# Step orders of a recurrent attention kernel laid anew, and the late pass of its first expert moved into the ordered part

## The chip, the cores and the metric

The kernel runs on one core of a Trainium2 chip. The metric is the device time of one execution in microseconds (us). The core has five engines with a queue each: TensorE (PE, matmuls; PEld is its loading of weights), VectorE (DVE), ScalarE (ACT), GpSimd (POOL) and SyncE (SP, which here only issues DMAs).

## The reference

Two blocks. The first is a recurrence over 768 tokens for 4 batches of 8 heads of 40 columns, the second sends each of the 3072 tokens through one of 8 experts:

```python
for t in range(S):
    y[:, :, t] = np.einsum('bhd,bhde->bhe', rt, state)
    Sa = np.einsum('bhde,bhe->bhd', state, at)
    state = state * wt[:, :, None, :] - np.einsum('bhd,bhe->bhde', Sa, bt) + np.einsum('bhd,bhe->bhde', vt, kt)
...
logits = x @ w_gate
expert_idx = np.argmax(logits, axis=1)
for e in range(E):
    h = np.maximum(x_sorted[lo:hi] @ w1[e], 0.0)
    y_sorted[lo:hi] = h @ w2[e]
return gate_w[:, None] * y_sorted[inv_perm]
```

All is float32. An expert has w1 of 320 x 1024 and w2 of 1024 x 320.

## The kernel before, in words

**Units.** The recurrence is done in chunks of 64 tokens. A unit is one chunk of two batches (16 heads), so there are 24 units, numbered 0 to 23. `unit(u)` lists its steps: loads of the six inputs (`load`, L793), two scans over the decays on DVE (`scan_r`, `scan_q`), the scaling of the inputs (`decay_kb`, `decay_a`), a product of the scaled inputs on PE (`p_a`), the inverse of a triangular matrix by repeated squaring (`p_sq`, `p_sum2`, `p_sum4`, `p_sum8`, `p_last`, with the copies `x0`, `x1`, `s1` and so on between them), the right-hand side and the solution (`p_rhs`, `p_first`, `p_q`, `p_u2`), the output and the new state (`p_z`, `p_y`, `sa`), and transposes on PE (`t_v`, `t_kb`, `t_gt`, `t_st`, `t_u`). `p_x` turns the output into rows of tokens and computes the gate's logits; the rows are scaled (`scaled`, `weight`) and written to `x_rows` in DRAM (`store`). A name with `:21` is that of unit 21; `/1` is the second step of that name in the unit.

**Routing.** Every few units `route` picks the expert of each token (`choose`), counts (`p_count`, `counts`, `place`) and builds a table of the tokens of each expert (`one_hots`, `p_table`, `tab`). From it come index tables: `rows_from` (where to gather rows) and `rows_to` (where to scatter results). `by_count` and `in_places` sort the experts 1 to 7 by size, which the fetch of weights after `order` needs.

**Expert 0 in the ordered part.** Expert 0 has room for 448 rows. Its first 256 are taken from the early chunks: gathered by two `rows_in` (POOL), transposed (`p_rows`, L1353, copied by `rows`), through layer 1 (`p_h`, `p_h3` for the last 64 input columns, `relu`) and layer 2 (`p_z0`), copied to `zo` and scattered by `rows_out` (L330). Six more `rows_in` gather the 192 late rows of expert 0 (`/2`, `/3`) and the rows of expert 1 (`/4` to `/7`).

**Order.** Each step is declared with its engine, its cost by the author's estimate, what it reads and writes, and `n`, the number of records that it puts into PE's queue (a matmul counts as two matmuls and two weight loads). `in_order()` (L483) then emits everything. On each engine the order is written out by hand: `FIRST_STEPS` for the start, `LAST_STEPS` for the end, and between them `CYCLE`, which gives each step a place relative to its unit, so that the same order comes back for each unit. The planner in `in_order` keeps a clock, which decides PSUM banks and how many dummy matmuls (`keep_warm`, L479) go into PE's gaps of the first 60 us and ahead of the labels in `KEEP`. It models PE's instructions as coming in pages of `PAGE` = 256 records, of which a new one may start `FETCH` us after the one before it at the earliest. Into these pages it counts only `n`.

**The second part.** After the ordered part its pool of buffers (`ring`) and its PSUM pool are given back, and the rest is scheduled by the framework: at its head the late pass of expert 0, `layer1` on the 192 late rows into `h_first` (L1461, L1469, L1475, L1476) and `layer2` of 128 of them (L1486, L1492); then experts 1 to 7, PE busy with layer 1 and layer 2 in turn, while POOL gathers the next experts' rows (`gathers`, L1439) and SP fetches their weights (L318, L320, L324). `wx`, one large tile, holds the X buffers of the ordered part and later the weights and rows of expert 1. `xg`, `h_first` and the weights of expert 2 lie where the ring was.

Of the kernel before, what the change touches and what calls it, by code (L numbers as in the profile page):

```python
# [23 lines left out]
def kernel(  # L24
# [249 lines left out]
    def rows_to_(v, t, tmp, gi, si):  # L274

        ta, tb, ia, ib = tmp
        v.tensor_scalar(ia, gi, scalar1=(B - 1) * C, scalar2=None, op0=ALU.bitwise_and)
        v.tensor_scalar(ib, gi, scalar1=(B * C).bit_length() - 1, scalar2=None, op0=ALU.arith_shift_right)
        v.tensor_copy(tb, gi)
        v.scalar_tensor_tensor(tb, in0=ia, scalar=float(NCH - 1), in1=tb, op0=ALU.mult, op1=ALU.add)  # L280
        v.scalar_tensor_tensor(tb, in0=ib, scalar=float(C - B * C), in1=tb, op0=ALU.mult, op1=ALU.add)

        v.tensor_scalar(ta, t, scalar1=0.0, scalar2=float(2 * N), op0=ALU.is_equal, op1=ALU.mult)
        v.tensor_tensor(si, tb, ta, op=ALU.add)
# [44 lines left out]
    def rows_out(zo, si, alone=False):  # L329
# [5 lines left out]
        if not alone:  # L335
# [8 lines left out]
    PAGE, FETCH, FIRST = 256, 3.6, 190  # L344
# [5 lines left out]
            t_v:0 t_kb:0 p_a:0 p_sq:0 t_v:1 t_kb:1 t_gt:0 p_sum2:0 p_a:1 p_sum4:0 p_sq:1 p_sum8:0 t_gt:1 p_rhs:0 p_last:0 p_sum2:1 p_q:0 p_a:2  # L350
            p_first:0 p_sum4:1 p_u2:0 t_u:0 p_sum8:1 p_z:0 p_rhs:1 p_last:1 p_sq:2 t_kb:2 p_y:0 p_sum2:2 p_q:1 p_first:1 t_gt:2 t_kb:3 p_u2:1 t_v:2
            p_sum4:2 t_u:1 p_a:3 p_z:1 p_sum8:2 p_sq:3 p_y:1 p_last:2 t_gt:3 p_x:0 p_rhs:2 p_sum2:3 p_q:2 p_first:2 p_x:1 p_u2:2 t_st:2 t_v:3
            p_sum4:3 p_a:4 t_u:2 t_kb:4 p_sum8:3 p_z:2 p_sq:4 p_last:3 t_v:4 t_st:3 p_rhs:3 p_y:2 t_v:5 p_sum2:4 p_q:3 t_kb:5 p_x:2
        """,
        DVE: """
            zero_dec zero/3 zero/1 zero_dec/1 scan_r:0 zero_dec/2 decay_kb/1:0 recip:0 scan_q:0 decay_a:0 scan_r:1 recip:1 decay_kb/1:1 n1:0 n1/1:0
            t1:0 scan_r:2 x0:0 s1:0 scan_q:1 decay_a:1 x02:0 s2/1:0 recip:2 n1:1 s2:0 n1/1:1 t1:1 x04:0 s4/1:0 s4:0 s1:1 scan_q:2 s8/1:0 x08:0 s8:0
            x0:1 direct/1:0 direct:0 apart:0 s2:1 decay_kb/1:2 s2/1:1 x02:1 n1:2 n1/1:2 t1:2 s4:1 x04:1 s4/1:1 scan_r:3 recip:3 x08:1 s8/1:1 s8:1
            zu/1:0 zu:0 scan_r:4 s1:2 x0:2 direct/1:1 direct:1 xt:0 x02:2 decay_kb/1:3 s2:2 s2/1:2 scan_q:3 scan_r:5 x04:2 s4/1:2 s4:2 n1/1:3 n1:3
            t1:3 zu/1:1 zu:1 s8:2 x08:2 s8/1:2 recip:5 xt:1 s1:3 kept/1:2 x0:3 recip:4 scan_q:4 x12/1:3 x02:3 s2:3 logits:0 logits:1 s2/1:3  # L360
            weight:0 weight:1 u/1:2 scaled:1 minus:2 s4:3 x04:3 x14/1:3 s4/1:3 n1:4 n1/1:4 t1:4 x08:3 s8/1:3 s8:3 zu:2 kept/1:3 zu/1:2 v:4 scan_r:6
            apart/1:3 s1:4 x0:4 sa:2 xt:2 scan_q:5 x12:4 nkb/1:5 s2:4 x02:4
        """,
        ACT: """
            zero/4 first_load/1:0 first_load/3:0 first_load/3:1 first_load/1:1 zero/5 zero/7 pc:0 zero/10 nkb/1:0 zero/8 nkb:0 pc:1 gt/1:0 zero/9
            gt:0 off/1:0 pc:2 v/1:0 v:0 x1:0 nkb/1:1 off:0 gk:0 x12/1:0 gt:1 x12:0 zero/6 nkb:1 gt/1:1 x14:0 x14/1:0 x1:1 off/1:1 off:1 v/1:1 rhs:0
            v:1 apart/1:0 x12:1 x12/1:1 q:0 gk:1 first:0 x14:1 minus:0 x14/1:1 off:2 u:0 ut:0 gt:2 off/1:2 gt/1:2 u/1:0 rhs:1 x1:2 nkb/1:2 nkb:2
            pc:3 apart:1 apart/1:1 sa0:0 x12:2 q:1 first:1 x12/1:2 gk:2 nkb:3 minus:1 nkb/1:3 v/1:2 ut:1 pc:4 v:2 x14/1:2 x14:2 u:1 gt:3 u/1:1
            off/1:3 gate/6 gt/1:3 x1:3 off:3 kept:2 sa0:1 gk:3 apart:2 apart/1:2 rhs:2 pc:5 q:2 first:2 x12:3 exp:0 exp:1 u:2 sn:2 v:3 v/1:3 x14:3
            scaled/1:1 scaled:0 gt:4 scaled/1:0 ut:2 off/1:4 gt/1:4 off:4 nkb/1:4 nkb:4 kept:3 x1:4 sn:3 rhs:3 v/1:4 apart:3 v:5 x12/1:4 q:3  # L370
        """,
        POOL: """
            zero/11 zero basis basis/1 zero/2 const gate const/1 basis/2 const/2 basis/3 basis/4 const/3 basis/5 basis/6 const/4 const/5 basis/7
            const/6 basis/8 basis/9 basis/10 basis/11 basis/16 basis/12 zero/12 decay_kb:0 const/7 basis/17 basis/13 const/8 zero/13 basis/14
            const/9 basis/15 const/10 const/11 blocks zero/19 basis/18 decay_kb:1 const/12 const/13 zero/15 const/14 gt_mask:0 basis/19 gate/1
            zero/17 zero/14 const/15 gate/2 const/16 gate/3 const/17 gt_mask:1 const/18 basis/20 const/19 const/20 const/21 decay_a:2 decay_kb:2
            basis/21 gate/4 gt_mask:2 const/22 const/23 zero/16 decay_kb:3 decay_a:3 const/24 zero/18 decay_kb/1:4 zero/20 const/25 st:2 gt_mask:3
            decay_kb:4 tt_add:2 decay_kb/1:5 decay_a:4 xs_pad:0 st:3 gt_mask:4 decay_kb:5 tt_add:3 decay_kb:6 decay_kb/1:6 decay_a:5 st:4 const/26
            xs_pad:1
        """,  # L380
        SP: """
            first_load:0 first_load/2:0 first_load/5:0 first_load/4:0 first_load:1 first_load/2:1 load:2 first_load/5:1 first_load/4:1 load/1:3
            load/2:2 load/3:2 load/1:2 load/3:4 first_load/6:0 load:5 load:3 gate/5 load/2:3 load:4 load/3:3 load/4:3 first_load/6:1 load/2:4
            load/4:2 load/1:4 load/1:5 load/5:2 load/2:6 load/1:6 load/4:4 load/2:5 load/3:5 load:6 load/4:5 load:7 store:0 load/5:3 load/2:7
            load/1:7 load/3:6 store:1 load:8 load/5:4
# [4 lines left out]
            t_gt:21 t_st:20 p_q:20 p_first:20 p_sum4:21 p_u2:20 p_a:22 p_sum8:21 t_u:20 p_x:19 p_z:20 p_last:21 p_rhs:21 t_gt:22 p_sq:22 p_y:20  # L390
            p_q:21 p_sum2:22 p_first:21 t_kb:23 p_u2:21 p_sum4:22 p_a:23 p_x:20 p_rhs:22 p_sum8:22 t_u:21 p_count:19 p_sq:23 p_last:22 p_z:21
            t_st:22 t_st:21 t_v:23 p_sum2:23 p_y:21 p_rows p_sum4:23 p_q:22 p_first:22 p_x:21 t_gt:23 p_u2:22 p_sum8:23 p_rhs:23 t_u:22 p_last:23
            t_st:23 p_z:22 p_q:23 p_first:23 p_u2:23 p_table:19 p_rows/1 t_u:23 p_y:22 p_z:23 p_h p_count:21 p_x:22 p_y:23 p_h/1 p_h/2 p_x:23
            p_h/12 p_h/13 p_h/3 p_count:23 p_h3 p_h/14 p_table:21 p_h/15 p_h/4 p_h/5 p_h/6 p_table:23 p_h/7 p_h3/1 p_h3/3 p_h/8 p_h/9 p_h/10 p_z0/8
            p_h/11 p_h3/2 p_z0 p_z0/1 p_z0/2 p_z0/9 p_z0/10 p_z0/3 p_z0/11 p_z0/12 p_z0/4 p_z0/5 p_z0/13 p_z0/6 p_rows/4 p_rows/3 p_z0/14 p_rows/5
            p_z0/7 p_rows/6 p_rows/2 p_z0/15 p_rows/7
        """,
        DVE: """
            x12/1:21 s2/1:21 x04:21 s4/1:21 s4:21 n1/1:22 n1:22 t1:22 s8:21 x08:21 s8/1:21 logits:19 zu/1:20 zu:20 kept/1:21 weight:19 apart/1:21
            x0:22 s1:22 xt:20 scan_q:23 x02:22 s2:22 s2/1:22 sa:20 s4:22 x04:22 n1/1:23 s4/1:22 n1:23 x14/1:22 t1:23 logits:20 s8/1:22 s8:22 x08:22  # L400
            x0:23 direct:22 direct/1:22 s1:23 zu/1:21 zu:21 weight:20 x12:23 s2:23 x02:23 s2/1:23 sa:21 xt:21 s4:23 x04:23 rows s4/1:23 x14/1:23
            s8:23 s8/1:23 x08:23 rhs:23 direct:23 direct/1:23 apart/1:23 sn:23 q:23 logits:21 zu/1:22 zu:22 choose:21 weight:21 scaled:21
            scaled/1:21 xt:22 zu/1:23 zu:23 place:21 logits:22 xt:23 one_hots:21 tab:19 logits:23 choose:23 weight:23 weight:22 place:23
            one_hots:23 tab:21 scaled:22 tab:23 rows_from:23 by_count:23 in_places:23 rows_from/1:23 rows/6 rows/2 zo rows_to:23 rows_to:15
        """,
        ACT: """
            apart:20 apart/1:20 nkb:22 v/1:22 x12:21 gk:21 v:22 q:20 first:20 sn:20 x14/1:21 x14:21 minus:20 u/1:20 u:20 ut:20 off:22 gt/1:22 gt:22
            off/1:22 kept:21 exp:19 rhs:21 scaled:19 gk:22 scaled/1:19 apart:21 pc:22 x1:22 q:21 x12:22 first:21 x12/1:22 minus:21 u:21 u/1:21
            nkb:23 nkb/1:23 x14:22 off:23 gt:23 rhs:22 gt/1:23 off/1:23 counts:19 ut:21 apart/1:22 x1:23 exp:20 sn:21 apart:22 scaled/1:20 sn:22
            x12/1:23 v/1:23 v:23 scaled:20 first:22 q:22 x14:23 gk:23 minus:22 ut:22 apart:23 first:23 minus:23 exp:21 ut:23 rows/1 exp:23 exp:22  # L410
            scaled/1:22 relu relu/1 scaled/1:23 scaled:23 relu/2 relu/6 relu/3 relu/4 relu/5 relu/7 rows/4 rows/5 rows/7 zo/1 rows/3
        """,
        POOL: """
# [1248 lines left out]
```

## Time and profile before

| | |
|---|---|
| median of 3 runs | 660.93 us (659.87 to 661.71) |
| the profiled execution | 665.98 us, span 664.2 us |
| mean granted PE clock | 0.992 |
| PE busy, 0 to 17, 17 to 60 us | 11.44 of 17, 36.23 of 43 us |
| PE busy, 100 to 400 us | 94.38, 95.19 and 94.47 us of each 100 |
| PE busy, 420 to 440, 440 to 460 us | 14.08 and 20.00 of 20 us, clock 0.87 and 0.96 |
| PE busy, 600 to 664.2 us | 56.37 of 64.2 us |
| instruction queue q8 | 105 packets, 1.72 MB |
| last matmul of the ordered part, first of expert 1 | before 431.6 us, at 447.39 us |

Times in the profile are from the start of the span. "x13256" is a count of instructions; in a timeline row the figures are start, duration, engine, line, operation, output and inputs, count, and in brackets the idle time before it with what ended it. "issue" is idle time in which the engine waited for nothing that the profile shows. PEclk is the clock that TensorE was granted, as a share of full speed.

### The profile page before, as it was taken

The page shows a single profiled execution, that of the slowest core. Times are in us where ns is not written, and L with a number is a line of the kernel's source. Part 1 is how long each engine was busy: PE and PEld are TensorE (multiplying, and loading weights), DVE is VectorE, ACT ScalarE, POOL GpSimd, SP SyncE. Part 2 cuts the span into 40 slices and gives each one's busy share as a digit, 9 for nine tenths or more (in the row PEclk, how much of TensorE's full clock was granted, in tenths as well). Part 3 has the DMA queues.
Part 4 walks back from the last instruction along what each step waited for, and adds up shares of the span by engine and source line. Part 5 has one row for each costly group of instructions (what it writes and reads, how often), then busy time and mean ns, then how long its engine had stood idle before and what let it go on. Part 6 is the DMA issues. An engine that isn't in the chain of part 4 may idle for free. (4 is left out here: it accounts for less than half of the span.)

```text
span 664.2 us, 30511 instructions
## 1 busy us (share of the span) xinstructions
PE 620.6 (93%) x13256; PEld 491.5 (74%) x13256; DVE 377.6 (57%) x906; ACT 291.1 (44%) x778; POOL 276.0 (42%) x426
## 2 busy tenths in 40 slices
PE   6699999999999999999999999789999999999995
PEld 6588888888898888888888887564656566555663
DVE  6898988778888888888887777312011201111110
ACT  5567666566676766676667542101010111101010
POOL 8625535565656465737565430250105013111101
PEclk9999999999999999999999999889999999999998
DMA  4433233233333434333332211764528212135000
GB/s 102 91 80 86 63 82 82 64 76 76 80 81 85 104 87 104 83 83 95 74 99 71 72 39 38 229 217 134 178 95 260 76 34 59 42 114 156 20 10 26
DMA packets 120189, 60.55 MB, mean 91 GB/s; under 512 B 100571, under 2 KB 115934, under 8 KB 120052
## 3 DMA queue, kind: packets, MB, share of 16 engines
q1 hardware_dynamic: 115036, 48.83, 27.9%
q0 software_dynamic: 2976, 9.24, 4.3%
q8 instruction: 105, 1.72, 1.1%
q10 hardware_dynamic: 2040, 0.49, 0.3%
q14 instruction: 32, 0.26, 0.1%
HBM read 49.88 MB, written 8.94 MB: 89 GB/s over the span
## 5 line engine op out<-in xcount | busy, mean ns | idle before, releaser
L1475 DVE TENSOR_SCALAR h_sb<-hp 128x416 f32<-128x416 f32 (+3 forms) x28 | 16.3, 582 | 164.8 <-PE hp L1469 141.6
L756 PE MATMUL ps<-wx 64*64 64x96 f32 (+1 forms) x3072 | 83.9, 241 | 5.0 <-issue 2.9
L330 POOL DMA_INDIRECT out_dram<-zo,s_idx x24 | 23.7, 988 | 143.8 <-ACT zo L1492 142.6
L756 PEld LDWEIGHTS ps<-wx 64*64 64x64 f32 x3072 | 68.4, 133 | 13.9 <-issue 5.6
L883 DVE TENSOR_TENSOR wx<-ps,wx 64x128 f32<-64x128 f32 (+1 forms) x216 | 61.7, 286 | 16.6 <-PE ps L756 11.2
L915 DVE STREAM_TRANSPOSE wx<-ps 128x512 f32<-128x512 f32 x72 | 51.1, 710 | 20.7 <-PE ps L756 17.3
L825 POOL TENSOR_TENSOR KB<-KB,rv 128x512 f32<-128x512 f32 x44 | 52.6, 1213 | 9.9 <-DMA KB<-in_packed_dram 4.5
L745 ACT COPY wx<-ps 128x256 f32<-128x256 f32 (+2 forms) x116 | 45.6, 419 | 25.1 <-PE ps L1353 13.1
L855 POOL TENSOR_TENSOR GT<-GT,m_low 128x512 f32<-128x512 f32 x24 | 30.6, 1277 | 58.7 <-ACT GT L853 29.1
L1492 ACT COPY zo<-zp 128x320 f32<-128x320 f32 (+1 forms) x24 | 10.2, 425 | 102.0 <-PE zp L1486 94.2
L1476 ACT ACTIVATE h_sb<-hp 128x416 f32<-128x416 f32 (+3 forms) x28 | 14.3, 509 | 86.5 <-PE hp L1469 43.5
L1486 PE MATMUL zp<-wx,h_sb 128*128 128x320 f32 (+3 forms) x176 | 48.5, 433 | 0.0
L1461 PE MATMUL hp<-xgT,w 128*128 128x416 f32 (+1 forms) x128 | 46.6, 512 | 0.0
L1486 PE MATMUL zp<-w,h_sb 128*128 128x320 f32 (+1 forms) x176 | 44.1, 433 | 0.0
L756 PE MATMUL ps<-ZU,nKB 128*64 128x104 f32 (+1 forms) x768 | 40.6, 254 | 2.6 <-issue 2.5
L1486 PEld LDWEIGHTS zp<-wx,h_sb 128*128 128x128 f32 (+3 forms) x176 | 30.5, 175 | 13.8 <-issue 0.7
L945 POOL TENSOR_TENSOR Tb<-Tb,wx 128x256 f32<-128x256 f32 x20 | 18.2, 908 | 51.2 <-ACT Tb L745 41.4
L1461 PEld LDWEIGHTS hp<-xgT,w 128*128 128x128 f32 x128 | 23.7, 190 | 21.2 <-issue 17.1
L756 PEld LDWEIGHTS ps<-ZU,nKB 128*64 128x64 f32 x768 | 34.6, 137 | 5.7 <-issue 4.1
L1486 PEld LDWEIGHTS zp<-w,h_sb 128*128 128x128 f32 (+1 forms) x176 | 28.8, 175 | 13.3 <-issue 0.7
L827 POOL TENSOR_TENSOR A<-A,q 128x512 f32<-128x512 f32 x22 | 26.9, 1222 | 24.8 <-DVE q L818 21.3
L818 DVE TENSOR_TENSOR_SCAN q<-dec,qini 128x520 f32<-128x520 f32 x24 | 35.9, 1496 | 0.2
(282 smaller groups left out, 1394.9 us busy)
## 6 DMA issues: line engine op xcount, KB each, us to landing
KB<-in_packed_dram SPq DMA_DIRECT2D x184, 40.0 KB
w<-in_moe_w_dram SPq DMA_DIRECT2D x10, 512.0 KB
w<-in_moe_w_dram SPq DMA_DIRECT2D x16, 320.0 KB
x_rows<-xs SPq DMA_DIRECT2D x24, 192.0 KB
Vu<-in_packed_dram SPq DMA_DIRECT2D x96, 40.0 KB
A<-in_packed_dram SPq DMA_DIRECT2D x96, 40.0 KB
R<-in_packed_dram SPq DMA_DIRECT2D x96, 40.0 KB
wx<-in_moe_w_dram SPq DMA_DIRECT2D x12, 320.0 KB
```

The lines of the kernel that those rows point to most:

```text
L330: ins_ = nc.gpsimd.indirect_dma_start(out=out[:, :], out_offset=bass.IndirectOffsetOnAxis(ap=si, axis=0), in_=zo, in_offset=None, bounds_c ...
L745: nc.scalar.copy(dst, src)
L756: nc.tensor.matmul(out_, lhsT=lhsT, rhs=rhs, start=start, stop=stop, skip_group_check=True)
L818: Step(turn_of("scan_q", pre - 1.0), DVE, 1.26, lambda e: nc.vector.tensor_tensor_scan(qq[:], dec[:, : SEG * C1], qi[:].rearrange("p s j - ...
L825: Step(turn_of("decay_kb", pre), on_, 1.2 if on_ == POOL else 0.65, lambda e, kb=kb, by=by: any_(e).tensor_tensor(kb, kb, by, op=ALU.mult) ...
L827: Step(turn_of("decay_a", pre), DVE if early else POOL, 0.65 if early else 1.2, lambda e: any_(e).tensor_tensor(Aq[:], Aq[:], q3[:, :, :C] ...
L855: Step(turn_of("gt_mask", rk), POOL, 1.28, lambda e, d=dst_, m=mask: nc.gpsimd.tensor_tensor(d, d, m, op=ALU.mult), reads=[h_basis], write ...
L883: nc.vector.tensor_tensor(dst[o_, q, :, 2, :HB], src[o_, q, :, 1, :HB], old[o, q, :, 2, :HB], op=ALU.add)
L915: Step(turn_of(f"x0{k}", rk - 0.4), DVE, 0.72, lambda e, ps=ps, Xn=Xn: nc.vector.transpose(Xn[:, :, :, 0, :], half_sums(ps, 2)[:, :, :, 0, ...
L945: Step(turn_of("tt_add", rk - 1.5), POOL, 0.72, lambda e, X=X, Tb=Tb: nc.gpsimd.tensor_tensor(Tb[:], Tb[:], X[:, :, :, 2, :HB], op=ALU.add ...
L1461: nc.tensor.matmul(hps[i][:, : c1 - c0], lhsT=w[0][:, db, (fb + i) * 128 : (fb + i + 1) * 128], rhs=xT[:, db, c0:c1], start=(db == 0 and n ...
L1486: nc.tensor.matmul(zp[r0 : r0 + n], lhsT=h[:, fb, c0 : c0 + n], rhs=w[2][:, fb, :], start=(fb == 0), stop=(fb == FB - 1), skip_group_check ...
```

## The change

1. **The page count.** `FETCH` goes from 3.6 to 3.7. The planner now also counts into the pages four records per dummy matmul, and the extra records of some steps (`MORE`).
2. **All step orders are new**: FIRST_STEPS, LAST_STEPS and CYCLE. In one unit PE did `p_last t_kb p_rhs t_v t_gt p_sum2 p_q p_first p_a p_u2 p_sum4 t_st t_u p_x p_z p_sq p_sum8 p_y`; it does `p_last t_kb t_v p_rhs p_sum2 p_q t_gt t_st p_first p_a p_u2 p_sum4 t_u p_x p_z p_sum8 p_sq p_y`. `counts` goes from ACT to DVE.
3. **The late pass of expert 0 becomes ordered steps**: `p_hb`, `p_hb3`, `relu_late` (two per block of 128 hidden columns), `p_zb`, `zo_late` and a third `rows_out`. Its hidden values go to `late_h`, over the second KB buffer, and for the 64 rows that wait for expert 1 to `h_tail` in `wx`. `h_first` is gone.
4. **`zo` of the early rows** moves from the ring's `rv` buffers to `wx`; `zo_late` lies over `turn_gate`.
5. **`rows_to` of the early rows** is cut into seven steps named `to`, declared when their table is ready instead of at the end.

The core of the diff, with the PE rows of the lists and the POOL and SP rows that matter:

```diff
-    PAGE, FETCH, FIRST = 256, 3.6, 190
+    PAGE, FETCH, FIRST = 256, 3.7, 190
+    MORE = {"t_v": 2, "p_a": 1, "p_sq": 1, "p_z": 2}
...
     FIRST_STEPS = {
         SP: """
-            first_load:0 first_load/2:0 first_load/5:0 first_load/4:0 first_load:1 first_load/2:1 load:2 first_load/5:1 first_load/4:1 load/1:3
+            first_load:0 first_load/2:0 first_load:1 first_load/4:0 first_load/2:1 load:2 first_load/5:0 first_load/4:1 load/1:2 load/2:2
...
     LAST_STEPS = {
         PE: """
-            t_st:23 p_z:22 p_q:23 p_first:23 p_u2:23 p_table:19 p_rows/1 t_u:23 p_y:22 p_z:23 p_h p_count:21 p_x:22 p_y:23 p_h/1 p_h/2 p_x:23
-            p_h/12 p_h/13 p_h/3 p_count:23 p_h3 p_h/14 p_table:21 p_h/15 p_h/4 p_h/5 p_h/6 p_table:23 p_h/7 p_h3/1 p_h3/3 p_h/8 p_h/9 p_h/10 p_z0/8
-            p_h/11 p_h3/2 p_z0 p_z0/1 p_z0/2 p_z0/9 p_z0/10 p_z0/3 p_z0/11 p_z0/12 p_z0/4 p_z0/5 p_z0/13 p_z0/6 p_rows/4 p_rows/3 p_z0/14 p_rows/5
-            p_z0/7 p_rows/6 p_rows/2 p_z0/15 p_rows/7
+            t_st:23 t_u:22 p_h p_h/1 p_h/2 p_q:23 p_first:23 p_count:21 p_h/3 p_h3 p_u2:23 p_z:22 t_u:23 p_table:19 p_h/12 p_h/13 p_z:23 p_y:22
+            p_y:23 p_h/8 p_x:22 p_h/9 p_table:21 p_h/10 p_h/4 p_x:23 p_h/5 p_h/6 p_h/14 p_h/11 p_count:23 p_h/7 p_h/15 p_h3/1 p_h3/3 p_h3/2 p_z0/8
+            p_table:23 p_z0/9 p_z0 p_z0/1 p_z0/10 p_z0/2 p_z0/11 p_z0/12 p_z0/13 p_z0/3 p_z0/4 p_z0/5 p_z0/6 p_z0/14 p_rows/3 p_rows/2 p_z0/15
+            p_z0/7 p_hb p_hb/1 p_hb/12 p_hb/4 p_hb/8 p_hb/5 p_hb/6 p_hb/7 p_hb/9 p_hb/10 p_hb/13 p_hb/14 p_hb/11 p_hb/2 p_hb/15 p_hb/3 p_hb3
+            p_hb3/1 p_hb3/2 p_hb3/3 p_zb p_rows/4 p_zb/1 p_zb/2 p_rows/5 p_zb/3 p_zb/4 p_rows/6 p_zb/5 p_zb/6 p_rows/7 p_zb/7
...
         POOL: """
-            rows_in/1 xs_pad:21 xs_pad:22 xs_pad:23 rows_in/3 rows_in/4 rows_in/5 rows_in/6 rows_in/7 rows_in/2 rows_out rows_out/1
+            xs_pad:20 xs_pad:21 xs_pad:23 xs_pad:22 rows_in/3 rows_in/2 rows_in/4 rows_in/7 rows_in/5 rows_in/6 rows_out/1 rows_out/2 rows_out
...
     CYCLE = {
-        "p_a": [(PE, -2.325)], "p_count": [(PE, 2.025)], "p_first": [(PE, -0.375)], "p_last": [(PE, -0.725)], "p_q": [(PE, -0.425)], "p_rhs": [(PE, -0.625)],
-        "p_sq": [(PE, -1.875)], "p_sum2": [(PE, -1.475)], "p_sum4": [(PE, -1.225)], "p_sum8": [(PE, -0.825)], "p_table": [(PE, 5.075)], "p_u2": [(PE, -0.275)],
+        "p_a": [(PE, -2.475)], "p_count": [(PE, 1.875)], "p_first": [(PE, -0.525)], "p_last": [(PE, -0.975)], "p_q": [(PE, -0.725)], "p_rhs": [(PE, -0.825)],
+        "p_sq": [(PE, -2.075)], "p_sum2": [(PE, -1.775)], "p_sum4": [(PE, -1.375)], "p_sum8": [(PE, -1.175)], "p_table": [(PE, 5.425)], "p_u2": [(PE, -0.425)],
...
-            left = s.n
+            warm = 0
+            if s.n and new and idle > 0.9 and (t < WARM or s.label in KEEP):
+                warm = int((idle - (0.6 if idle < 8 else 3.0)) / 0.3)
+            left, done = s.n, -4 * warm - MORE.get(s.name, 0) if s.n else 0
...
-            while left:
+            while left or done:
...
             if c1 == EC:
-                later.append(found(0, tab_a[:], g0_idx[:], s0_idx[:], [h_tab_a]))
+                found(0, tab_a[:], g0_idx[:], s0_idx[:], [h_tab_a])
+                for part in rows_to_parts(nc.vector, tab_a[:], [x[:, :NA] for x in tmp], g0_idx[:], s0_idx[:]):
+                    Step(turn_of("to", rk), DVE, 0.18, lambda e, part=part: part(), reads=[h_idx[0], h_tab_a], writes=[h_to[0], h_itmp])
...
-                later.pop()()
...
+        h_tail = wx[:, : FB * (CAP - EW - 128)].rearrange("x (k r) -> x k r", k=FB)
...
-        zo0 = [(t[:, :Dm], held) for t, held in r_rv.bufs]
+        late_h = flat(r_KB.bufs[1][0]).rearrange("x (k r) -> x k r", k=FB)
+        zo_late, hzo_late = flat(turn_gate)[:, :Dm], [h_tg]
+        zo0 = [(wx[:, tail_w + i * Dm : tail_w + (i + 1) * Dm], [part_of(r_X.bufs[0][1])]) for i in range(NA)]
...
+        for fb in range(0, FB, 2):
+            ps = Held(2)
+            for i in range(2):
+                for db in range(DB - 1):
+                    Step(late + 2, PE, 0.33, lambda e, ps=ps, fb=fb + i, i=i, db=db: mm(
+                        psum[:, ps.at + i, : CAP - EW], w0[0][:, db, fb * 128 : (fb + 1) * 128], xT0[:, db, EW:], start=(db == 0), stop=False,
+                    ), reads=hxT_late + [h_w], writes=[ps], n=4, lag=0, shape=WHOLE, name="p_hb")
...
+            if j == NA:
+                for fb in range(FB):
+                    Step(late + 3, PE, 0.54, lambda e, ps=ps, fb=fb: mm(
+                        psum[:, ps.at, :Dm], late_h[:, fb], w0[2][:, fb, :], start=(fb == 0), stop=(fb == FB - 1),
+                    ), reads=late_parts[0][fb : fb + 1] + [h_w], writes=[ps], n=4, shape=WHOLE, lag=0.2 if fb + 1 == FB else 0, name="p_zb")
+                Step(late + 3, ANY, 0.42, lambda e, ps=ps: copy(e, zo_late, psum[:, ps.at, :Dm]), reads=[ps], writes=hzo_late, name="zo_late")
+                Step(late + 3, POOL, 1.2, lambda e: rows_out(zo_late, s_idx[:, NO - 1 : NO]), reads=hzo_late + [h_to[2]], lag=2.5, name="rows_out")
+                continue
...
-    hs[0] = wk_pool.tile([128, FB, CAP - EW], F32, name="h_first", bufs=1)
-    layer1(weights[0], xTs[0], hs[0], EW, CAP, to=0)
-    layer2(rows_to(0, 0), (weights[0], hs[0], 0, 128))
```

## The prediction

> **What bounds the kernel now.** First the page's busy shares and the time in 40 slices, then the windows by stage: TensorE (PE) is busy 93% of the span, 284 of the 300 us from 100 to 400, and all of 440 to 600. The other engines stay under 60%. So time can come only from PE's own gaps and from its slow clock.
>
> ```profile
> PE 620.6 (93%) x13256; PEld 491.5 (74%) x13256; DVE 377.6 (57%) x906; ACT 291.1 (44%) x778; POOL 276.0 (42%) x426
> ```
>
> Second, who PE waits for in the ordered stage (60 to 400 us):
>
> ```profile
> PE ps L756 <- issue: 11.6, 26, 1.2
> PE ps L756 <- ACT wx L745: 1.5, 9, 0.2
> ```
>
> "issue" means that no semaphore held it. The timeline shows where:
>
> ```profile
> 204.93 0.48 PE L756 MATMUL ps<-ZU,nKB 128*64 128x104 f32 x5 [0.47 <-issue]
> 212.80 0.83 PE L756 MATMUL ps<-x,Q 64*64 64x40 f32 x22 [0.79 <-issue]
> ...
> 228.24 0.90 PE L756 MATMUL ps<-x,Q 64*64 64x40 f32 x25 [0.23 <-issue]
> ```
>
> The gaps fall inside a step, between equal matmuls. From 204.93 to 212.80 there are about 254 matmul records and as many weight loads, so two pages of 256 in 7.87 us; the later gaps at 236.41, 244.05, 251.96 and 259.71 are again about 7.8 us apart. PE is waiting for its instructions, in one page of every two. How much that is per unit:
>
> ```profile
> 107.74 1.09 PE L984 MATMUL ps<-ident,KB 128*128 128x128 f32 x8
> 348.36 1.09 PE L984 MATMUL ps<-ident,KB 128*128 128x128 f32 x8
> ```
>
> This step comes once per unit: 15 units in 240.62 us, 16.04 us each. Third, the end of the ordered stage:
>
> ```profile
> 419.47 2.85 PE L756 MATMUL ps<-w,dec 128*128 128x320 f32 x10
> 425.04 1.54 PE L1353 MATMUL ps<-ident,q 128*128 128x128 f32 x6 [2.71 <-DMA q<-x_rows,g_idx]
> ...
> 431.61 1.57 PE L1461 MATMUL hp<-xT,w 128*128 128x192 f32 x8 [0.96 <-ACT xT L745]
> ...
> 437.74 2.37 PE L1461 MATMUL hp<-xT,w 128*128 128x192 f32 x8 [2.21 <-ACT h_first L1476]
> ...
> 443.08 4.47 PE L1486 MATMUL zp<-w,h_first 128*128 128x320 f32 x16
> 447.39 3.17 PE L1461 MATMUL hp<-wx 128*128 128x448 f32 x8
> ```
>
> Three stops, and after two of them the same 192-column step takes 2.37 us instead of 1.57. The granted clock says why (in the windows, the figure after the length and five busy times: 0.67, 0.50, 0.59):
>
> ```profile
> 424.00:426.00 2.00, 0.96 (x5) 0.96 (x6) 0.00 (x0) 0.02 (x1) 0.00 (x0) 0.67 1.05 370
> 426.00:428.00 2.00, 2.00 (x8) 1.50 (x7) 0.00 (x0) 0.46 (x1) 0.00 (x0) 0.50 1.01 351
> ...
> 438.00:440.00 2.00, 2.00 (x8) 1.60 (x7) 0.33 (x2) 0.00 (x0) 1.70 (x2) 0.59 0.78 248
> ```
>
> What the third stop waits for is in the chain and on GpSimd (POOL): row scatters from rv start only after the last index chain of VectorE (DVE), and h_first lies where the ring was, so its first write waits until the second scatter has read rv.
>
> ```profile
> 434.43 1.00 DMA out_dram<-rv,s_idx
> 435.43 1.62 issue
> ```
> ```profile
> 433.10 1.03 POOL L330 DMA_INDIRECT out_dram<-rv,s_idx  x1 [10.14 <-DVE s_idx L284]
> ```
>
> **The late pass (p_hb, p_hb3, p_zb).** Before, PE's last early matmul ends at 422.32 and expert 1 starts at 447.39: 25.07 us. The same work by its warm rows, start to start: six p_rows at 0.45 = 2.7; three p_z0 at 0.54 = 1.6; layer 1 of 192 columns 4 x 1.50 = 6.0; its third part 2 x 0.85 = 1.7; layer 2 447.39 - 443.08 = 4.3; sum 16.3. The last evacuation (zo_late, 0.42 like the other zo copies, with its hand-over about 0.7) now stands ahead of the first hp, which takes the banks. 17.0, so 8.1 us can go. The other edits here cost no PE time: rows_to in seven DVE pieces of 0.16 us leaves the end of the chain for gaps far earlier, zo moves to wx, so nothing of the ring waits for a scatter.
>
> What is late next. (a) All sixteen p_h now stand ahead of p_table:23, and p_x:23 has ten p_h and one p_h3 before it instead of three p_h: about 4 us later, at 410.3 for 406.3. The index chain, the gathers of experts 0's late rows and 1's rows and the 2.56 MB fetch of expert 1 (issued 414.60 to 419.7, DMA full until 428.5) shift with it, to about 432.5. Expert 1 would start near 440, its transposes p_rows/4 to 7 near 434: covered by p_hb and p_zb; without that cover this would be a wait of up to 4 us. (b) p_rows/3 and /2 now stand ahead of p_hb. Their two gathers are now the first on POOL, ahead of the weights in time (about 417 to 419 against 420). Bounds: nothing, if they land as free transfers; 4.6 us, if rows_in/2 takes the 7.1 us that rows_in/4 took (issued 416.91 to 417.9, used at 425.04 in a full DMA). I take 1.0, nearer nothing, since their issue is ahead. (c) On POOL rows_out/2 stands ahead of rows_out and of the seven gathers of experts 2 and 3; it waits for zo_late. They start near 443 instead of 437.93, 3 us after expert 1's start instead of 9.5 ahead of it. PE wants the first four 15.8 us after that start (463.22 - 447.39), they are issued by 448 and may take 7.1 us: about 1.5 us of slack. The Trainium skill (DMA: Bandwidth & Descriptors, the arbitration rule of the queue model) has each engine take turns between its queues, packet by packet, which would bring them in 2 to 3 us, a cost of nothing; the 7.1 us row would eat the slack. I take 0.5, bounds 0 and 3. DVE and ScalarE (ACT) have 16 small relus more in the list, but they stand for the eight of h_first (0.33 to 0.36 each), while PE has p_zb; nothing.
> Late pass: 25.1 - 17.0 - 1.5 = **-6.6** (bounds -8.1 and -0.5).
>
> **The step orders.** The set of PE steps per unit is unchanged, 1024 records and by the new table 6 more; only the sequence changes. Durations start to start from 216.23 to 231.73: p_z 1.16, p_sq 0.68, p_sum8 0.66, p_y 2.04 (its 0.47 stall out), p_last 0.60, t_kb 1.02, p_rhs 1.07, t_v 0.49, t_gt 0.53, p_sum2 0.72, p_q 0.46, p_first 0.44, p_a 0.90, p_u2 0.80, p_sum4 0.70, t_st 0.49, t_u 0.45, p_x 1.00: 14.2 us, against 16.04 measured. Cut into pages of 256 from p_z on, the old order takes 2.50, 4.06, 3.09 and 4.56 us. If no page may follow in less than 3.7 us (the new FETCH; two pages at 7.64 to 7.9 us in the trace allow it), the unit is 3.7 + 4.06 + 3.7 + 4.56 = 16.0. That meets the trace. The new order, cut from p_rhs on: 2.25 (p_rhs, p_sum2, p_q), 3.69, 3.69, 4.58, so 15.7. Where the cut falls drifts by 6 records per unit; slid through the unit, the old order gives 15.6 to 15.9, the new one 15.0 to 15.9. The gain is thus from 0.7 down to a loss of 0.3 us per unit. The skill speaks against any: Runtime: NRT & Kernel Launch, Instruction fetch mechanics, has pages of 256 fetched ahead and the fetch hidden, since instructions are dispatched more slowly than they come. By that rule this part is worth 0; by the gap rows, which sit at page distance, it isn't. I follow the rows, but take only 0.2 us per unit, since other waits (1.5 us for ACT's wx) take up part of it: 17 units between the two lists, **-3.4** (bounds -12 and +5).
>
> At the start, the load of A moves ahead on SyncE's (SP) queue by about 2 us. DVE's decay_a waits for it:
>
> ```profile
> 11.78 0.69 DVE L827 TENSOR_TENSOR A<-A,q 128x512 f32<-128x512 f32 x1 [2.02 <-DMA dec<-in_packed_dram]
> ```
>
> and PE's first p_a (12.53) for that. Between 0 and 1.5 us; other waits stand close, so **-0.5**. DVE, ACT, POOL and SP keep their work in other orders; they are busy at most 90% of any long window (DVE), the copy of the counts that goes from ACT to DVE is 0.2 us every fourth unit, and waits on them cost PE about 5 us in 340. I count nothing, bounds -2 and +2, in the range.
>
> **Sum.** -6.6 - 3.4 - 0.5 = -10.5. The profiled execution took 666.0 us (span 664.2) and would take 655.5; the median of the runs is 660.9, 0.8% less, so 650.4.
>
> **Rivals.** Pages are not what holds PE, or the drift eats it: only the late pass and the start count, 660.9 - 7.1 = 653.8. For it: the rule above; the stalls are 11.6 us of named gap, less than my 1.8 per unit. Against: their spacing.
> The gathered rows come late: 4.6 at p_rows/2 and 3 at expert 2's transposes, 7.6 instead of 1.5, each followed by a slow clock: the late pass gives 1 and pages 2, about 658.
> The orders fit better than I take: 0.6 per unit, 643.6.
> Slower: the new order's dense run p_rhs, p_sum2, p_q is 256 records in 2.25 us, denser than anything before (2.5). If page starts stay on it, and its neighbours aren't thin where I cut them, it costs 3.7 - 2.25 = 1.45 us in each unit, and p_first, p_u2 and p_a behind it a second stall. It decides from 7.1 / 17 = 0.42 us per unit on; at 0.6 it is 660.9 - 7.1 + 10.2 = 664. Against it: the cut that I did gives no such sum.
> The change doing nothing is excluded: the 25 us stretch is rebuilt.
>
> **Chances.** 0.3% is 2 us, about what a measurement of this kernel can tell from no change. Likeliest case 0.50 (650.4, itself 647 to 654), only the late pass 0.22, better orders 0.09, late rows 0.12 (a third of it within 2 us), slower 0.07. Faster 0.50 + 0.22 + 0.09 + 0.07 = 0.88, same 0.05, slower 0.07. The range leaves out most of the slower and late-row cases and the best tenth: 644.5 to 657.5.
>
> **What would show it.** Right: no wait for scatters of rv and no clock under 0.9 after 425; expert 1's first hp 17 to 19 us after the last early p_z0 block; t_kb to t_kb 15.6 to 15.9 us; fewer issue gaps. Wrong: a DMA wait before p_rows/2 or before expert 2's transposes, t_kb spacing at 16.0 or above, or the first hp held by zo_late for more than 1 us.

## The result, and the profile after

| | before | after |
|---|---|---|
| median of 4 runs | 661.32 us | 653.05 us |
| ratio, 95% interval | | 0.9873 (0.9839 to 0.9907) |
| profiled execution, span | 665.98, 664.2 us | 654.40, 652.7 us |
| first matmul of expert 1 | 447.39 us | 435.39 us |
| from there to the end of the span | 216.8 us | 217.3 us |

650.4 was forecast, in a range of 644.5 to 657.5. The profiled execution of before lay 4.7 us above the median of its runs, that of after 1.4 us above; so the profiled executions differ by 11.6 us and the medians by 8.3. Measured twice more, on chip 10, the ratio of the same two kernels was 0.9785 (0.9758 to 0.9812) and 0.9809 (0.9759 to 0.9859). The gain is 1.3 to 2.2%, by set of runs.

Busy shares, from the page of after:

```profile
PE 618.0 (95%) x13254; PEld 491.6 (75%) x13254; DVE 372.1 (57%) x907; ACT 295.8 (45%) x785; POOL 267.7 (41%) x426
```

PE does the same work, 2.6 us less of it, and idles 9 us less. The end of the ordered part of after, from the timeline of PE:

```profile
418.30 2.32 PE L772 MATMUL ps<-w,dec 128*128 128x320 f32 x8
420.46 0.82 PE L1382 MATMUL ps<-ident,q 128*128 128x128 f32 x6
421.11 1.24 PE L772 MATMUL ps<-w,dec 128*128 128x320 f32 x4
422.19 5.36 PE L772 MATMUL ps<-xT,w 128*128 128x192 f32 x32
427.48 1.57 PE L772 MATMUL ps<-xT,w1c 64*128 64x192 f32 x16
428.99 0.81 PE L772 MATMUL ps<-w,KB 128*128 128x320 f32 x2
...
434.18 0.70 PE L772 MATMUL ps<-w,KB 128*128 128x320 f32 x2
435.39 3.27 PE L1520 MATMUL hp<-wx 128*128 128x448 f32 x8 [0.52 <-ACT turn_gate L761]
```

All three stops are gone. p_rows/3 and /2 (L1382, 420.46) start where the block before them ends, p_hb follows at 422.19, and the one wait left is 0.52 us for zo_late, which lies over turn_gate. From the start of p_rows/3 to expert 1 there are 14.93 us; with the one p_z0 that the prediction's count has and this stretch hasn't (0.54), 15.5, where before took 25.07. The windows of after, in which the figure after the length and the five busy times is the granted clock:

```profile
424.00:426.00 2.00, 2.00 (x14) 2.00 (x14) 0.00 (x0) 0.00 (x0) 1.19 (x2) 1.00 1.07 365
426.00:428.00 2.00, 2.00 (x16) 1.77 (x16) 0.00 (x0) 0.00 (x0) 0.00 (x0) 1.00 1.03 361
...
438.00:440.00 2.00, 2.00 (x10) 0.69 (x8) 0.19 (x1) 0.18 (x1) 1.39 (x3) 1.00 0.97 291
```

The DMA engines are as full as before (shares 1.07 and 1.03), but PE works through it and keeps its clock at 1.00. On POOL:

```profile
414.93 1.08 POOL L1373 DMA_INDIRECT q<-x_rows,g_idx  x1 [3.71 <-DVE key L227]
416.32 1.07 POOL L1373 DMA_INDIRECT q<-x_rows,g_idx  x1 [0.30 <-issue]
...
435.73 0.98 POOL L1498 DMA_INDIRECT xg<-x_rows,g_idx  x1 [10.24 <-ACT turn_gate L761]
437.02 1.02 POOL L334 DMA_INDIRECT out_dram<-turn_gate,s_idx  x1 [0.30 <-issue]
```

rows_in/2, issued by 417.39, was there when PE took it up at 420.8. One gather of experts 2 and 3 goes ahead of the scatter of zo_late, the other six from 439.65 to 446.9; PE takes them at 451.33 without a wait.

In the units the picture is less plain. The same step in two units, and who PE waited for from 60 to 400 us:

```profile
109.86 1.09 PE L1000 MATMUL ps<-ident,KB 128*128 128x128 f32 x8
348.75 1.09 PE L1000 MATMUL ps<-ident,KB 128*128 128x128 f32 x8
```
```profile
PE ps L772 <- issue: 13.5, 30, 1.6
PE ps L772 <- ACT TT L966: 0.7, 2, 0.5
```

15 units in 238.89 us, 15.93 each for 16.04. The wait for ACT's wx (1.5 us) has gone, the issue gaps are 13.5 us for 11.6. By 404.65 us unit 23 has its p_y done, as before (404.30), but about 3.1 us more of expert 0's p_h and p_h3 has been done by then. So in these two traces the orders and the start give about 2.8 of the 12.0 us by which expert 1 starts earlier, and the rest, 9.2, comes after.

### The profile page after: what moved, and what is told of

It reads as the page before. It is cut to its first block, busy times and chain, and to the rows that moved or that the text cites. A ratio compares the mean times of both kernels' runs of the same rounds, so it can differ in the third digit from the quotient of the medians.

```text
span 652.7 us, 30589 instructions
## 1 busy us (share of the span) xinstructions
PE 618.0 (95%) x13254; PEld 491.6 (75%) x13254; DVE 372.1 (57%) x907; ACT 295.8 (45%) x785; POOL 267.7 (41%) x426
## 4 chain that ended last, share of the span: by engine, by line
PE 55%; issue 29%; POOL 6%; DVE 4%; DMA 2%; SPq 2%; ACT 1%; POOLq 0%; DVEq 0%; ACTq 0%
PE ps L772 45%; PE ps L881 7%; POOL out_dram L334 4%; PE ps L1000 3%; POOL xg L1498 2%; DVE ZU L1085 2%; SPq L809 2%; DMA Vu<-in_packed_dram 1%; DMA A<-in_packed_dram 1%; DVE wx L899 0%; DMA KB<-in_packed_dram 0%; DMA dec<-in_packed_dram 0%; PE ps L1382 0%; DVE wx L931 0%; ACT TT L966 0%
## 5 line engine op out<-in xcount | busy, mean ns | idle before, releaser
L772 PE MATMUL ps<-wx 64*64 64x96 f32 (+1 forms) x3072 | 87.5, 241 | 5.4 <-issue 3.4
L772 PEld LDWEIGHTS ps<-wx 64*64 64x64 f32 x3072 | 70.1, 133 | 12.1 <-issue 6.1
L841 POOL TENSOR_TENSOR KB<-KB,rv 128x512 f32<-128x512 f32 x44 | 55.2, 1256 | 18.5 <-DVE rv L828 8.3
L761 ACT COPY wx<-ps 128x256 f32<-128x256 f32 (+3 forms) x118 | 45.3, 420 | 19.8 <-PE ps L772 9.1
L1535 ACT ACTIVATE h_sb<-hp 128x416 f32<-128x416 f32 (+3 forms) x28 | 14.3, 509 | 88.1 <-PE hp L1528 41.8
L1498 POOL DMA_INDIRECT xg<-x_rows,g_idx x19 | 18.2, 957 | 44.7 <-PE tp L1506 29.6
L1016 POOL TENSOR_TENSOR ST<-sa,pc 128x320 f32<-128x320 f32 x22 | 15.9, 723 | 49.6 <-DVE sa L1107 49.6
```

The costliest lines, as they stand in the source:

```text
L761: nc.scalar.copy(dst, src)
L772: nc.tensor.matmul(out_, lhsT=lhsT, rhs=rhs, start=start, stop=stop, skip_group_check=True)
L841: Step(turn_of("decay_kb", pre), on_, 1.2 if on_ == POOL else 0.65, lambda e, kb=kb, by=by: any_(e).tensor_tensor(kb, kb, by, op=ALU.mult) ...
L1498: nc.gpsimd.indirect_dma_start(out=xg, out_offset=None, in_=x_d[:, :], in_offset=bass.IndirectOffsetOnAxis(ap=gi, axis=0),)
```

## The experiments

The theory: the end gives most of it, by taking away three stops and their slow clock; the orders give a little; where a page of PE's instructions starts within the unit decides part of the time. The first rival: end and orders share the gain evenly. The second: instructions are fetched ahead and hidden, so the pages don't matter. The runs come in three sets: the first on chip 7, the second and third on chip 10, each with before beside them. Each kernel is an edit of before or of after; none changes what is computed.

**First set. The end alone, e1_tail**: after, with the FIRST_STEPS and CYCLE of before (the PE rows of CYCLE are shown).

```diff
     CYCLE = {
-        "p_sq": [(PE, -2.075)], "p_sum2": [(PE, -1.775)], "p_sum4": [(PE, -1.375)], "p_sum8": [(PE, -1.175)], "p_table": [(PE, 5.425)], "p_u2": [(PE, -0.425)],
+        "p_sq": [(PE, -1.875)], "p_sum2": [(PE, -1.475)], "p_sum4": [(PE, -1.225)], "p_sum8": [(PE, -0.825)], "p_table": [(PE, 5.075)], "p_u2": [(PE, -0.275)],
...
```

> The changed kernel with the FIRST_STEPS and CYCLE lists of the kernel before: late pass, zo, index pieces and LAST_STEPS new, the orders of the start and of the repeated units old. Theory (the end of the ordered part gives most of it; from the last early matmul block to expert 1 the traces give 9.6 us, the orders 2.4): 652 to 653 against 661.3, t_kb to t_kb at 16.0 us. Rival (orders and end share the gain evenly): 657.

650.33 us against 659.00, ratio 0.9855 (0.9822 to 0.9887): 9.6 us by the ratio and 8.7 by the medians, about what the theory expected (8.3 to 9.3) and twice the rival's 4.3.

**The orders alone, e2_orders**: before, with the FIRST_STEPS and CYCLE of after (the same edit the other way).

> The kernel before with only the new FIRST_STEPS and CYCLE lists, its end as it was. Theory: 659 to 661.3, a gain of 0 to 2.4, t_kb to t_kb about 15.9 us instead of 16.04. Rival (the orders bring 0.2 us per unit and the start 0.5, as predicted): 657.4.

655.89 us, 0.9960 (0.9938 to 0.9983): 2.6 us. That is the theory's top end and below the 3.9 us of the prediction, but the interval, 1.1 to 4.1 us, holds both.

The new page count (point 1 of the change) is in e1_tail and not in e2_orders. With the same lists PE runs the same number of dummy records with it and without it (56 with the old lists, 54 with the new), so it gave nothing by way of the dummies.

**One edit of the end, e3_zo_in_wx**: before, with zo out of the ring.

```diff
-        zo0 = [(t[:, :Dm], held) for t, held in r_rv.bufs]
+        tail_w = FB * (CAP - EW - 128)
+        zo0 = [(wx[:, tail_w + i * Dm : tail_w + (i + 1) * Dm], [part_of(r_X.bufs[0][1])]) for i in range(NA)]
```

> The kernel before with one edit: zo of the early rows lies in wx instead of rv, so nothing of the ring is read by a scatter. Theory (h_first waits only for the scatter's reading of rv): the 2.2 us stop before 437.7 and the slow clock after it (1.6 us in three rows) go, 657.5. Rival (it waits for the scatter because the hand-over of the ring waits for all of POOL's or DVE's last work): no change, 661.3.

659.19 us, 0.9999 (0.9977 to 1.0020): no gain, and yet the theory's stop is gone. The 657.5 of the theory is missed; the rival named the time, but not the reason. The timeline of PE:

```profile
419.37 0.88 PE L1359 MATMUL ps<-ident,q 128*128 128x128 f32 x6 [2.46 <-DMA q<-x_rows,g_idx]
...
423.17 0.55 PE L1359 MATMUL ps<-ident,q 128*128 128x128 f32 x3 [0.89 <-DMA q<-x_rows,g_idx]
...
425.55 2.93 PE L1467 MATMUL hp<-xT,w 128*128 128x192 f32 x8 [0.96 <-DVE idx_tmp L283]
428.41 1.17 PE L1475 MATMUL hp<-xT,w1c 64*128 64x192 f32 x8
429.51 2.87 PE L1467 MATMUL hp<-xT,w 128*128 128x192 f32 x16
432.31 0.91 PE L1475 MATMUL hp<-xT,w1c 64*128 64x192 f32 x6
434.33 0.59 PE L1475 MATMUL hp<-xT,w1c 64*128 64x192 f32 x2 [1.11 <-issue]
434.85 1.57 PE L1467 MATMUL hp<-xT,w 128*128 128x192 f32 x8
```

The late pass runs through its second half without the wait for the scatter, and POOL starts the next gathers at 425.42. But ahead of it PE still stops for gathered rows (2.46 and 0.89 us in this trace), so now its first half runs on the slow clock (2.93 us for a step of 1.57), and an issue gap of 1.11 us comes in its middle. From the last early block to expert 1 it is 24.0 us (416.90 to 440.90), for 25.07 in the trace of before. Most of the time freed by one stop went to the next ones; e1_tail, which takes all three away, gains. The other two stops were not taken away one by one.

**Half a page more, e5_shift128**: after, with 128 more records in PE's queue at the start. Behind the dummies PE's work is the same.

```diff
     def keep_warm(bank, times):
+        if not shifted:
+            shifted.append(1)
+            times -= 6
+            for i in range(38):
+                nc.tensor.matmul(bank[:8, :8], lhsT=ident[:, :8], rhs=ident[:, :8], start=True, stop=True, skip_group_check=True)
         for i in range(times):
```

> The changed kernel with half a page (128) more records in PE's queue at the start: 6 of the dummy matmuls of the first gap are left out and 38 tiny ones (8 columns) put in. Nothing else of the work differs. Theory (PE waits for pages of 256, and where they start in the unit decides): t_kb to t_kb differs from 15.91 by 0.2 us or more, the time by 3 us or more, either way. Rival (instructions are fetched ahead and hidden): the same within 1.5 us, the start's delay at most 1 us of it.

646.60 us, 0.9801 (0.9766 to 0.9836). Its first t_kb starts at 10.28 us (9.97 in after's trace). The units come 15.61 us apart, against 15.93, more than the 0.2 us of the theory; but without any shift a trace of after's orders can have 15.54 (last section). After itself didn't run beside it: its interval meets that of e1_tail in the same set, so by itself this run shows no effect of the 128 records.

**Second set. The pages, e6_after_again, e5_shift64 and e5_shift192**: after as it is, and with 64 (3 dummies out, 19 tiny ones in) and 192 (9 out, 57 in) more records.

> The changed kernel as it is, beside the next ones on one chip. All theories: a ratio to before of 0.984 to 0.991, as first measured.

> The changed kernel with 64 more records in PE's queue at the start (3 dummies out, 19 tiny ones in). Theory (the start of the pages in the unit decides, and moves the time over a range of some 5 us): between the changed kernel and the one with 128 more, 0.981 to 0.988 of before. Rival (pages are fetched ahead and hidden; the gain of the 128 was that of its start alone): equal to the changed kernel within 0.2%.

> The changed kernel with 192 more records at the start (9 dummies out, 57 tiny ones in). Theory (pages): past the best start, so slower than with 128 again, 0.983 to 0.990 of before. Rival (fewer dummies or an earlier start gave the gain, and more of it gives more): below 0.980.

After 649.03 us, 0.9785 (0.9758 to 0.9812), a little better than was expected. With 64 more 644.83 us, 0.9702 (0.9670 to 0.9734); with 192 more 647.18 us, 0.9762 (0.9737 to 0.9788). Both shifts came out below the ratios that the theory had named, as after itself did, so they are read beside after; the rival's "below 0.980" for the 192 is met by after too. The 64 give 0.85%, 5.5 us by the ratios, where "hidden" says nothing; the 192 can't be told from after. So it isn't "more is better". The start doesn't hold the 5.5 us: the first three t_kb begin at 11.18, 15.91 and 25.51 us in e6_after_again and at 10.13, 15.53 and 24.63 in e5_shift64, the fourth at 45.27 and 46.33. PE's waits from 60 to 400 us, of e6_after_again and of e5_shift64:

```profile
PE ps L772 <- issue: 11.9, 24, 1.3
```
```profile
PE ps L779 <- issue: 6.6, 12, 0.9
```

Half as many gaps, 5.3 us less. That is where the shift was aimed, but it is one trace of each, and e4_gather_last below, with after's lists and no shift up to there, has 7.7 us. The times show that the 64 records matter; that they do so through fewer gaps is likely and not shown.

That the gaps are stops for instructions can be read from the kept traces themselves. They hold the packets of queue q8, 16 KB each, one about every 3.9 us; and PE's matmuls and weight loads can be counted in order. In the fourteen traces together there are 313 issue gaps of PE between 60 and 400 us. 297 of them end at a record whose number, counted from 0, leaves 193 or 194 when divided by 256 (23 of 26 in before, 28 of 30 in after, 14 of 14 in e5_shift64), and all of these end 1.19 to 1.75 us after a packet of q8 has landed. So pages of 256 records are real, and PE does wait for them.

**The gathers' order, e4_gather_last**:

```diff
-rows_in/3 rows_in/2 rows_in/4 rows_in/7 rows_in/5 rows_in/6 rows_out/1
+rows_in/3 rows_in/4 rows_in/7 rows_in/5 rows_in/6 rows_in/2 rows_out/1
```

> The changed kernel with the gather rows_in/2 of expert 0's last late rows at the end of POOL's six gathers, as in the kernel before, instead of second. Theory (behind the weights of expert 1 it lands 7 us after its issue): PE stops before p_rows/2 for 5 to 8 us, the clock falls for some 3 us after it, and the time is 6 to 9 us longer than the changed kernel's. Rival (the DMA engines take turns between queues, so it lands in 2 to 3 us): a stop of 2 to 3 us and 2 to 4 us in all.

660.61 us, 0.9956 (0.9933 to 0.9980): 1.71% or 11.3 us more than after in the same set, beyond both. From its timelines of POOL and PE, and its windows:

```profile
414.22 0.94 POOL L1373 DMA_INDIRECT q<-x_rows,g_idx  x1 [0.30 <-issue]
```
```profile
420.25 0.87 PE L1382 MATMUL ps<-ident,q 128*128 128x128 f32 x3 [9.57 <-DMA q<-x_rows,g_idx]
420.92 2.34 PE L772 MATMUL ps<-w,dec 128*128 128x320 f32 x4
423.05 6.49 PE L772 MATMUL ps<-xT,w 128*128 128x192 f32 x32
```
```profile
414.00:416.00 2.00, 0.00 (x0) 0.00 (x0) 0.00 (x0) 0.00 (x0) 0.94 (x1) 0.77 1.06 362
416.00:418.00 2.00, 0.00 (x0) 0.00 (x0) 0.00 (x0) 0.00 (x0) 0.00 (x0) 0.50 1.05 369
...
422.00:424.00 2.00, 2.00 (x6) 1.60 (x5) 0.00 (x0) 0.71 (x2) 0.00 (x0) 0.50 0.00 0
```

PE stood for 9.57 us: 3.5 until the gather was issued at all, 0.9 for the issue, 5.1 until it landed, most of that in full DMA engines. Then the same rows took 0.87, 2.34 and 6.49 us for 0.49, 1.24 and 5.36 at full clock, 2.6 us more. 9.6 + 2.6 = 12.2 us, near the 11.3. Of the theory the landing was right in kind (7 us expected, 5.1 seen); what it left out is that a gather at the end of the list also starts late.

**Third set. The whole and its parts side by side: e7_after_third, e7_tail_again, e7_orders_again**, the kernels of above once more.

> The changed kernel as it is, beside the next three on one chip. All theories: a ratio to before between 0.978 and 0.988, as in the two measurements so far.

> As e1_tail (new late pass and LAST_STEPS, old FIRST_STEPS and CYCLE), now beside the changed kernel. Theory (the end gives nearly all): within 0.3% of the changed kernel. Rival (the new orders of the units give 4 us, as predicted): 0.6% slower than the changed kernel.

> As e2_orders (new FIRST_STEPS and CYCLE, old end), now beside the changed kernel. Theory: 0.996 of before, and the two parts add up to the whole within 0.4%. Rival (they work only together, since the new end was laid for the new orders): the two gains fall short of the whole by over 0.5%.

The whole 651.54 us, 0.9809 (0.9759 to 0.9859); the end alone 655.92 us, 0.9889 (0.9849 to 0.9928); the orders alone 661.08 us, 0.9968 (0.9944 to 0.9991). The end gives 1.1% and the orders 0.3%, of 1.9% in all: what is over, 0.5%, lies within the intervals, and so it decides neither for parts that add up (within 0.4%) nor for parts that work only together (over 0.5%). "Nearly all" is too much said: here the end alone is 0.8% slower than the whole, and so nearer to the rival's 0.6%; in the first set it was as fast, by the ratio, as the whole in its own first measurement. Both parts gain; the end gains the greater part in both sets. The 0.3% of the orders can't be parted from the place of the pages: new lists put other steps at the page starts, and moving the starts alone moves the time by 0.85%.

**The pages of the old orders, e8_before_shift64**: before, with 64 more records (the same edit).

> The kernel before with 64 more records in PE's queue at the start (3 dummies out, 19 tiny ones in). Theory (where pages start in the unit matters for any order, and the old orders were laid without the six extra records per unit): a change of 0.3% or more, either way. Rival (only the new orders have a good place for the pages): within 0.3% of before.

666.42 us, 1.0041 (1.0019 to 1.0063), a change of 0.3% or more, as the theory expected. The same 64 records that make the new orders 0.85% faster make the old ones 0.4% slower. Its issue gaps from 60 to 400 us, and those of e7_tail_again (old orders, no shift) on the same chip:

```profile
PE ps L764 <- issue: 17.2, 24, 1.5
```
```profile
PE ps L771 <- issue: 13.0, 24, 1.8
```

17.2 us is the most of the five traces with the old orders (8.8 to 13.0 in the other four).

That the fetch is hidden is refuted for these step orders: the gaps sit at the page starts, and the count of records ahead of the units moves the time, both ways. Why 64 records help one order and hurt the other stays open (next section).

## Why the prediction was right

- **The sum owes something to luck.** Forecast -10.5 us in all, measured by the medians -8.3, and on chip 10 -14.3 and -12.2. The late pass was put too small and the orders too large, and the two errors offset each other.
- **The late pass: right in mechanism, 1 to 3 us too small.** Forecast -6.6, in the traces -9.6 (25.07 to 15.5), alone -9.6 and -7.4 us by the ratios. Two terms of the sum were mis-sized. The work was counted at 17.0 and took 15.5: sixteen p_hb in a row take 5.29 us, not 6.0, the third part 1.5 for 1.7, six p_rows 2.0 for 2.7. And the deductions of 1.0 for p_rows/2 and 0.5 for expert 2's rows were nothing. For p_rows/2 that is due to the gather's place in POOL's list: at the end of it the whole gain but 0.4% is gone.
- **What is late next.** (a) The shift of the index chain was forecast as 4 us and was about 2 (p_x:23 at 407.44 for 405.27); the weights of expert 1 were issued from 417.15 on, 2.6 us later, and their transfer ended near 430 for 432.5: covered, as said. (c) The gathers of experts 2 and 3 came in time, and one of them even ahead of the scatters.
- **The stop for the scatter** was put down to the lifetime of rv. e3 shows that this reading was right and that the stop, taken away alone, was worth nothing that could be measured.
- **The step orders and the start: right in sign, probably too large.** Forecast -3.4 and -0.5, together -3.9; measured alone -2.6 and -2.1 us, with intervals of 1.1 to 4.1 and 0.6 to 3.7. The step of 0.2 us per unit isn't shown: the two traces give 15.93 for 16.04, four traces with the old orders and no shift 15.77 to 16.04, six with the new 15.43 to 15.98; the means differ by 0.14, and executions of one order by more. The issue gaps were not fewer.
- **The start.** At t_kb:7 after was even 2 us behind (109.86 for 107.74), though its first p_a had been 1.6 us ahead (10.94 for 12.53). Part of that is this one execution: in after's trace the clock is granted at 0.50 from 37.69 to 41.10 us, in before's nowhere between 8.3 and 424 us. e6_after_again, the same kernel, has no such stretch and reaches t_kb:7 at 106.45.
- **The tally of pages** was not the proof that it looked like. Slid through the unit, its durations give 15.2 to 16.0 us for the old order and 14.8 to 16.0 for the new, wider than the prediction has them. The records counted in the traces now say where the cut falls. With it the tally gives, as an estimate over 15 units, 15.7 us per unit for the old order, 15.2 for the new and 15.5 for the new with 64 more records: for the orders a gain of some 8 us, where 2 to 3 were measured, and for the 64 records a loss, where 5.5 us were gained. So pages stop PE, but "no page in less than 3.7 us" is not enough to say what an order costs; through which wait the new orders gain their 2 us is left open.
- **The rule of the Trainium skill** (Runtime: NRT & Kernel Launch, Instruction fetch mechanics: fetch hidden behind dispatch) was weighed against the gaps, and the gaps were followed. The 297 gaps at page starts and the shifts by 64 records bear that out: the measurement decides against the rule here. The 2 to 3 us that the prediction drew from the turns of the DMA queues were not seen in e4_gather_last: that gather took 5.1.
- **The rivals.** "Only the late pass" named 653.8 and the median was 653.05, by accident: the orders do count, and the late pass counts for more. Late rows and the slower case, a loss through the dense run of p_rhs, p_sum2, p_q, did not come.
- **The signs.** No wait for scatters of rv and a clock of 1.00 behind 425 us came as said. Expert 1 came sooner than said (14.8 us after the last early block, for 17 to 19), the spacing of 15.93 lies just outside 15.6 to 15.9, and fewer issue gaps did not come (30 for 26). None of the signs of being wrong came.

**A better version**: e5_shift64 beats both kernels, 644.83 us on its chip, 2.98% under before and, by intervals that don't meet, under after. It is the best of three shifts that were tried, measured once.

## What to carry to other kernels

Count what the sequencer must fetch as a resource: where a gap falls between equal instructions and nothing holds the engine, look at how far apart the gaps are, and try a few dozen harmless records at the start before laying orders anew. When stops follow each other on one engine, look at them together: here one taken away alone handed its time to the next, at a slower clock. When work is moved forward to fill a wait, its inputs must move in their queue as well; here the place of one gather was worth 11.3 of the 14.3 us that the whole change gave on that chip.

## What the runs showed of the hardware

Executions of the same code differ mainly in the issue gaps. After, e6_after_again and e7_after_third are one kernel, e4_gather_last the same up to the last 35 us of the ordered part; their issue gaps from 60 to 400 us were 13.5, 11.9, 15.3 and 7.7 us, their spacing of units 15.93, 15.98, 15.96 and 15.54 us.

Packets of q8 took 0.88 to 1.85 us each in before's trace from 60 to 400 us, so the time to fetch a page isn't constant. Timed runs of one kernel on one chip spread as well (before on chip 7: 654.4 to 662.6). One trace can't tell 0.1 us per unit. What makes a fetch slow in one execution was not tried.

The start differs for another reason. The first 42 dummy matmul records take 6.56 us in after and 7.75 us in e6_after_again:

```profile
3.58 6.56 PE L491 MATMUL ps<-ident 128*128 128x128 f32 x42 [3.58 <-POOL ident masks.py:199]
```
```profile
3.58 7.75 PE L491 MATMUL ps<-ident 128*128 128x128 f32 x42 [3.58 <-POOL ident masks.py:199]
```

Behind the first one, each lasts 421 ns at first and 275 ns later, and the kept traces have their first record of the full clock there: at 6.97 us in one and 9.48 in the other. No packet of q8 moves before 15.99 us in either. From there to the last 25 us of the span the slow clock comes in fixed pieces: at 0.50 for 3.41 us twice in before, once in after and once in e3_zo_in_wx, and in e4_gather_last for 10.24, three times as long, beginning within the stop of 9.57 us.
